# Moving deferred stores from ScalarE's to SyncE's queue, and cutting GpSimd's 1024-column sums in two

## The chip, the cores and the metric

The kernel runs on one core of one Trainium2 chip. The metric is device time in microseconds (us) of that core. A profile of one execution goes with each kernel. All runs that are compared here are of the fast state; the granted TensorE clock is told where it matters.

The engines' names: TensorE is PE in the profile (its weight loads PEld), VectorE is DVE, ScalarE ACT, GpSimd POOL, SyncE SP. "SPq" and "ACTq" are the sequencers of SyncE and ScalarE, which issue the DMAs, in order: when one issue waits, the later ones stand behind it (12.3 us at SyncE in the changed kernel). A DMA lands when its data have arrived; in the kernel before, the 718 DMAs of SyncE landed in the order of their issue, and so did the 202 of ScalarE. In this program TensorE writes its results into PSUM; a bank is a part of PSUM, which VectorE or ScalarE reads out before the program lets TensorE use it again. The other tiles lie in SBUF. The profile also tells the clock that TensorE was granted, as a share of full speed; a stretch at 0.5 is called a half-clock stretch here (in own_by_scalar matmuls stood 0.42 us apart in one, in place of 0.216).

## The reference, cut to what matters

Two blocks follow each other. A lightning attention with decay over (4, 8, 768, 64) gives x of 3072 tokens by 512. Then four experts work on every token:

```python
p = domain_probs / (domain_probs.sum(-1, keepdims=True) + 1e-09)
for e in range(4):
    h = np.maximum(x @ w1[e], 0.0)        # 512 -> 1024
    out += p[:, e:e + 1] * (h @ w2[e])    # 1024 -> 512
```

All is float32. The expert products are over 95% of the multiplications.

## The kernel before

The products are made by Winograd's form of Strassen's scheme, partly in two levels: seven products of sums of blocks in place of eight products. So sums of blocks of x, w1 and w2 ("operands") are needed. They are made once, on GpSimd and VectorE, stored to DRAM tensors (`x_ops`, `w1_ops`, `w2_sums`, `w2_ops`), and loaded again for each group of tokens. Three groups (`g`) of 1024 tokens times four experts make twelve units; a unit has seven first products (x with w1) and seven second ones (hidden with w2), whose matmuls alternate on TensorE.

Work that is not urgent goes through two queues in the program: `chores` make sums, and `stores` holds the DMAs that write them. A store is issued two pumps after its sums were put into the program, so that its data should be ready by then:

```python
def pump():
    for f in older:
        f()
    older[:] = stores
    stores.clear()
    if chores:
        chores.pop(0)()
```

The stores are on ScalarE's queue (one of several places):

```python
s = stage.tile([P, 4, 256], FP32, name="ops", tag="st")
for i, (name, x, y, op) in enumerate(ops):
    b[name] = s[:, SLOT[name]]
    tt(eng, b[name], b[x], b[y], op)              # 4 sums of 256 columns
stores.append(lambda: (
    nc.scalar.dma_start(out=to[:, 0], in_=blk[:, 0, 0:256]),
    nc.scalar.dma_start(out=to[:, 1:5], in_=s[:]),
    nc.scalar.dma_start(out=to[:, 5:7], in_=blk[:, 1].rearrange("p (a f) -> p a f", a=2)),
    made.add(what),
))
```

ScalarE also copies TensorE's results out of PSUM and applies the Relu. The loads are on SyncE's queue (`nc.sync`), written into the program one product ahead; `xs_in` and `ws_in` have two buffers each, `w2t` six. The outer sums of w1, w2 and x are one GpSimd instruction of 1024 columns each:

```python
def total(name, a, b, op):
    t = stage.tile([P, 2, W], FP32, name="w1o", tag="st")   # W = 512
    tt(nc.gpsimd, t[:], st[a][:], st[b][:], op)
    st[name] = t
```

For the first group and the second expert (seven pairs of operands) the sums are both stored and used at once by TensorE; `keep_own` makes these stores, three for x and three for w1 in each pair, 42 DMAs. I call them the own stores.

## Time and profile before

| | before |
|---|---|
| median of the first 3 runs | 1215.12 us (1214.82 to 1217.88) |
| span of the profiled run | 1211.4 us |
| TensorE busy | 1186.9 us, 98% |
| VectorE, ScalarE, GpSimd busy | 66%, 22%, 51% |
| DMA issues by SyncE and by ScalarE | 718 and 202 |
| TensorE's gaps over 0.15 us, summed | 20.8 us, of these 9.7 us from 53 to 669 us |

Two views carry the reading: TensorE's waits (who waited, for whom, us in total, times, longest) and the timeline around each wait. The prediction shows their lines. With TensorE at 98%, the busy shares of the others say nothing of what an edit is worth; the list of TensorE's few gaps does.

### The profile page before, as it was taken

Reading aid. Unit: us, or ns where it says so; the run is one execution under the profiler, and the core shown is the slowest. Engines: PE = TensorE matmul, PEld = TensorE weight load, DVE = VectorE, ACT = ScalarE, POOL = GpSimd, SP = SyncE. Lnnn points to the kernel's source line nnn. Section 1 sums busy time; section 2 is a strip of 40 time slices with the busy share of each in tenths; the row PEclk is TensorE's granted clock in tenths of the full one; section 3 lists DMA queues with packets and bytes.
Section 4 is the critical chain, followed back from the end, with each engine's and each line's share of the span. In section 5 each row is a group of like instructions: output and inputs, shape, how many; then the busy total and the mean of one; then the engine's idle time right before and its main releaser. Section 6 shows DMA issues by size and latency. Waiting matters only on the chain.

```text
span 1211.4 us, 17782 instructions
## 1 busy us (share of the span) xinstructions
PE 1186.9 (98%) x6593; PEld 1024.2 (85%) x6593; DVE 802.2 (66%) x1313; ACT 261.7 (22%) x476; POOL 622.8 (51%) x548
## 2 busy tenths in 40 slices
PE   7999999999999999999999999999999999999998
PEld 6788888888888888888888888888888888888877
DVE  5587686478567846746764874764665667777774
ACT  3322112112212211321211120120143241241132
POOL 4556247466366800015624655405665774873873
PEclk9999999999999999999999999999999999999999
DMA  9578489999999875679987998988986657566542
GB/s 234 155 274 270 168 279 316 367 311 317 350 338 320 282 264 188 221 246 292 293 288 239 293 315 318 333 288 258 326 301 235 238 202 268 198 258 209 204 170 74
DMA packets 227446, 317.93 MB, mean 262 GB/s; under 512 B 91648, under 2 KB 168864, under 8 KB 227360
## 3 DMA queue, kind: packets, MB, share of 16 engines
q1 hardware_dynamic: 191840, 257.08, 64.3%
q10 hardware_dynamic: 35520, 59.72, 13.4%
q8 instruction: 52, 0.85, 0.3%
q14 instruction: 34, 0.28, 0.1%
HBM read 231.40 MB, written 85.34 MB: 261 GB/s over the span
## 4 chain that ended last, share of the span: by engine, by line
PE 89%; DVE 5%; DMA 2%; SPq 1%; ACT 1%; issue 0%; POOL 0%; ACTq 0%; DVEq 0%
PE pg L701 38%; PE q L755 30%; PE pq L926 13%; DVE m L94 2%; PE sp L455 2%; PE op L483 2%; PE op L478 1%; PE pM L1016 1%; DVE hS L94 1%; DVE xt L94 1%; SPq L110 1%; PE kp L432 1%; PE op L491 1%; PE qp L432 1%; PE pM L896 1%
## 5 line engine op out<-in xcount | busy, mean ns | idle before, releaser
L701 PE MATMUL pg<-xs_in,ws_in 128*128 128x256 f32 x1960 | 473.7, 382 | 3.2 <-DVE m L94 2.5
L701 PEld LDWEIGHTS pg<-xs_in,ws_in 128*128 128x128 f32 x1960 | 367.4, 190 | 62.2 <-DVE m L94 9.9
L94 DVE TENSOR_TENSOR m<-pg,m 128x512 f32<-128x512 f32 x451 | 307.6, 688 | 134.1 <-PE pg L701 122.4
L755 PE MATMUL q<-w2t,hS 128*128 128x256 f32 x1024 | 242.5, 380 | 0.0
L755 PEld LDWEIGHTS q<-w2t,hS 128*128 128x128 f32 x1024 | 193.9, 190 | 26.7
L771 DVE SCALAR_TENSOR_TENSOR acc<-q,gate,acc 128x256 f32<-128x256 f32 x192 | 92.5, 482 | 147.6 <-PE q L755 147.1
L755 PE MATMUL q<-w2t,m 128*128 128x256 f32 x768 | 181.7, 379 | 0.0
L755 PEld LDWEIGHTS q<-w2t,m 128*128 128x128 f32 x768 | 145.4, 190 | 20.0
L713 ACT ACTIVATE m<-m 128x512 f32<-128x512 f32 x132 | 82.9, 632 | 348.2 <-DVE m L94 308.2
L94 POOL TENSOR_TENSOR kn<-kn,s_decay 128x512 f32<-128x512 f32 x20 | 21.5, 1074 | 204.7 <-PE kp L432 193.3
L94 POOL TENSOR_TENSOR m<-m,xT 128x512 f32<-128x512 f32 x64 | 81.2, 1288 | 73.9 <-ACT m L713 52.3
L94 DVE TENSOR_TENSOR sums<-pq,sums 128x256 f32<-128x256 f32 x154 | 64.6, 422 | 46.8 <-PE pq L926 41.9
L926 PE MATMUL pq<-acc,w2t 128*128 128x256 f32 x352 | 86.6, 379 | 0.0
L94 DVE TENSOR_TENSOR m<-m,m 128x512 f32<-128x512 f32 x96 | 84.6, 887 | 0.0
L709 ACT COPY m<-pg 128x512 f32<-128x512 f32 x88 | 51.0, 587 | 141.9 <-PE pg L701 128.9
L926 PEld LDWEIGHTS pq<-acc,w2t 128*128 128x128 f32 x352 | 66.7, 190 | 9.6 <-issue 0.6
L94 POOL TENSOR_TENSOR ops<-w2b 128x256 f32<-128x256 f32 x24 | 17.4, 745 | 98.3 <-DMA w2b<-in_moe_w_dram 66.9
L648 ACT ACTIVATE m<-m 128x512 f32<-128x512 f32 x48 | 30.4, 632 | 149.0 <-DVE m L94 149.0
L94 POOL TENSOR_TENSOR acc<-hT,hT 128x512 f32<-128x512 f32 x32 | 40.2, 1271 | 30.8 <-PE pq L926 21.4
L94 DVE TENSOR_TENSOR hS<-m,m 128x512 f32<-128x512 f32 x64 | 49.6, 779 | 5.6 <-ACT m L713 5.6
L94 POOL TENSOR_TENSOR w2o<-w2b 128x1024 f32<-128x1024 f32 x16 | 39.6, 2480 | 19.2 <-DMA w2b<-in_moe_w_dram 9.6
L94 POOL TENSOR_TENSOR ops<-w1o 128x256 f32<-128x256 f32 x32 | 29.7, 947 | 30.1 <-PE pg L701 20.5
(126 smaller groups left out, 1328.4 us busy)
## 6 DMA issues: line engine op xcount, KB each, us to landing
xs_in<-x_ops SPq DMA_DIRECT2D x70, 896.0 KB, 5.0
ws_in<-w_ops SPq DMA_DIRECT2D x70, 896.0 KB, 8.1
w2t<-w_ops SPq DMA_DIRECT2D x66, 256.0 KB, 6.9
w2t<-w_sums SPq DMA_DIRECT2D x64, 256.0 KB, 5.2
w_ops<-ops ACTq DMA_DIRECT2D x28, 512.0 KB, 5.5
w2t<-in_moe_w_dram SPq DMA_DIRECT2D x48, 256.0 KB, 5.0
x_ops<-ops ACTq DMA_DIRECT2D x17, 512.0 KB, 7.8
w2b<-in_moe_w_dram SPq DMA_DIRECT2D x32, 256.0 KB, 5.9
```

The source lines that it names most:

```text
L94: eng.tensor_tensor(out=o, in0=a, in1=b, op=op)
L110: nc.sync.dma_start(out=to[:, :, r], in_=of[:, :, r])
L432: nc.tensor.transpose(out=x[:, ac * C:(ac + 1) * C], in_=y[:, 2 * ac:2 * ac + 2].rearrange("p r d -> p (r d)"), identity=ident[:],)
L455: nc.tensor.matmul(out=sp[r][:, ac * C:(ac + 1) * C], lhsT=hc(kT)[half[r], ac], rhs=hc(qT)[half[r], ac], start=True, stop=True,)
L483: nc.tensor.matmul(out=op[r][half[x], a * C:(a + 1) * C], lhsT=vn[:, 4 * r + 2 * a + x], rhs=hc(st[r])[:, 2 * a + x], start=(first and a = ...
L648: nc.scalar.activation(out=o[:], in_=o[:], func=AF.Relu)
L701: nc.tensor.matmul(out=p[:, j * 256:(j + 1) * 256], lhsT=ws[i][:, j * P:(j + 1) * P], rhs=xs[i], start=(fresh and j == 0), stop=True, skip ...
L709: nc.scalar.copy(out=new[at][:], in_=p[:])
L713: nc.scalar.activation(out=new[at][:], in_=new[at][:], func=AF.Relu)
L755: nc.tensor.matmul(out=p[:, s * DH:(s + 1) * DH], lhsT=h[A_OF[m]][:, c * 256 + s * P:c * 256 + (s + 1) * P], rhs=fed2[g, e, m][uu][:, c], ...
L771: nc.vector.scalar_tensor_tensor(out=o, in0=x, scalar=w, in1=o, op0=ALU.mult, op1=ALU.add)
L926: nc.tensor.matmul(out=p[:, 0:256], lhsT=fed3[e, m, x // 2][:, x % 2, c * P:(c + 1) * P], rhs=b[B_OF[i]][:, c * 256:(c + 1) * 256], start= ...
```

## The change

The intent: ScalarE should not issue stores, because its copies stand behind them, and a VectorE sum should not take 2.60 us beside a GpSimd sum where it takes 0.68 us alone. All deferred stores go to SyncE, and 52 GpSimd sums of 1024 columns become 104 of 512.

```diff
+    def halves(o, a, b, op):
+        for i in range(2):
+            tt(nc.gpsimd, o[:, i], a[:, i], b[:, i], op)
...
         stores.append(lambda: (
-            nc.scalar.dma_start(out=to[:, 0], in_=blk[:, 0, 0:256]),
-            nc.scalar.dma_start(out=to[:, 1:5], in_=s[:]),
-            nc.scalar.dma_start(out=to[:, 5:7], in_=blk[:, 1].rearrange("p (a f) -> p a f", a=2)),
+            nc.sync.dma_start(out=to[:, 0], in_=blk[:, 0, 0:256]),
+            nc.sync.dma_start(out=to[:, 1:5], in_=s[:]),
+            nc.sync.dma_start(out=to[:, 5:7], in_=blk[:, 1].rearrange("p (a f) -> p a f", a=2)),
             made.add(what),
         ))
...
-            tt(nc.gpsimd, t[:], st[a][:], st[b][:], op)
+            halves(t[:], st[a][:], st[b][:], op)
...
-                nc.scalar.dma_start(out=to[:, x:y], in_=of)
+                nc.sync.dma_start(out=to[:, x:y], in_=of)
```

Cut here: the same two edits at the sums of w2 and x, at the stores of `w2_sums` and at those of the finished rows of `out`.

More of the change, by code (lines that the diff above doesn't have):

```diff
@@ L223, in total @@
             flat = [x[:].rearrange("p u c d -> p (u c d)") for x in (t, st[a], st[b])]
-            tt(nc.gpsimd, *flat, op)
+            halves(*(x[:].rearrange("p u c d -> p u (c d)") for x in (t, st[a], st[b])), op)
             stores.append(lambda: (
-                nc.scalar.dma_start(out=w2_sums[e, n].rearrange("p u w -> p (u w)"), in_=flat[0]),
+                nc.sync.dma_start(out=w2_sums[e, n].rearrange("p u w -> p (u w)"), in_=flat[0]),
                 made.add(("w2", e, name)),
@@ L271, in total @@
             t = stage.tile([P, 2, 2, DH], FP32, name="w2o", tag="st")
-            tt(nc.gpsimd, *(x[:].rearrange("p q c d -> p (q c d)") for x in (t, st[a], st[b])), op)
+            halves(*(x[:].rearrange("p q c d -> p q (c d)") for x in (t, st[a], st[b])), op)
             st[name] = t
@@ L289, in total @@
             t = stage.tile([P, 2, W], FP32, name="xo", tag="st")
-            tt(nc.gpsimd, t[:], a, b, op)
+            halves(t[:], a, b, op)
             st[name] = t[:]
@@ L772, in part @@
             if e == E - 1 and m in ("M2", "M4", "M5", "M3"):
-                stores.append(lambda: nc.scalar.dma_start(out=out[n * P:(n + 1) * P, j * DH:(j + 1) * DH], in_=o))
+                stores.append(lambda: nc.sync.dma_start(out=out[n * P:(n + 1) * P, j * DH:(j + 1) * DH], in_=o))
         def done():
```

## The prediction

> **What bounds the kernel now.** I read the page's part 1 and part 5 first, then the waits of TensorE, then the timeline at each place where TensorE stands still.
>
> ```profile
> PE 1186.9 (98%) x6593; PEld 1024.2 (85%) x6593; DVE 802.2 (66%) x1313; ACT 261.7 (22%) x476; POOL 622.8 (51%) x548
> ```
>
> TensorE is busy for 1186.9 of 1211.4 us. Its mark of "busy" is no illusion here: I took the distance from one 128x256 matmul to the next in the trace, and 4808 of about 4960 are 0.21 to 0.22 us. So at most 24.5 us (2.0% of the span) can be won by any change that leaves the matmuls alone, and this one does: the order of instructions on TensorE holds the same work before and after. Adding up the gaps over 0.15 us in TensorE's timeline gives 20.8 us. Of them 7.8 us lie before 26 us (the first loads, two of the copies), and 3.2 us after 1156 us (the tail); the change touches neither. 9.7 us are left between 53 and 669 us. What ends each gap, from the waits of TensorE:
>
> ```profile
> PE pg L701 <- DVE m L94: 4.8, 6, 1.7
> PE pg L701 <- ACT m L709: 2.8, 2, 2.1
> PE pM L1016 <- DVE xt L94: 1.2, 1, 1.2
> ```
>
> Columns: waiter and what it waited for, us in total, times, longest. ScalarE and VectorE are 22% and 66% busy and yet late at these moments: something else holds them up. Two pieces of timeline show what. First the largest stall, in the chain of waits of the stretch 92 to 104 us (start, length, what):
>
> ```profile
> 95.30 0.33 ACT m L1028
> ...
> 98.09 0.48 ACTq L995
> 98.56 0.05 issue
> 98.61 1.15 ACT m L1028 x2
> 99.76 0.48 ACT m L709
> 100.24 0.14 issue
> 100.38 1.97 PE pg L701 x8
> ```
>
> ScalarE issues six stores in a row (0.33 to 0.72 us each), and the two Relus and the PSUM copy that TensorE needs stand behind them. TensorE idles 2.14 us. Then one of VectorE's, in the timeline of 241 to 249 us:
>
> ```profile
> 244.02 2.34 POOL L94 TENSOR_TENSOR w1o<-w1b 128x1024 f32<-128x1024 f32 x1
> ...
> 244.31 2.60 DVE L94 TENSOR_TENSOR m<-m,m 128x512 f32<-128x512 f32 x1
> ...
> 246.84 1.27 DVE L94 TENSOR_TENSOR m<-pg,m 128x512 f32<-128x512 f32 x2
> 247.57 1.59 PEld L701 LDWEIGHTS pg<-xs_in,ws_in 128*128 128x128 f32 x8 [0.77 <-DVE m L94]
> ```
>
> The same VectorE sum takes 0.68 us when GpSimd is quiet. Here it starts 0.3 us after a GpSimd sum of 1024 columns and ends 0.55 us after that one ends; the next VectorE operation, which frees TensorE's bank, is late.
>
> [...] ScalarE's 202 issues take 97 us, 0.48 us each. [...]
>
> **The change part by part.** Stores: 195 of ScalarE's 202 issues go to SyncE (718 become 913 in the built order). ScalarE gets back about 195 x 0.48 = 94 us of sequencer time, nearly all beside other work. On TensorE's path I count:
> - the stall at 98.2 us, 2.1 us, goes;
> - at 200.7 us a copy from PSUM stands behind a store that waited for GpSimd: 0.6 us, goes;
> - at 185.6 us the chain is stores, late copy of qT at 182.15, VectorE's qs, late m: 0.6 us, goes.
> Together 3.3 us.
>
> Halves: GpSimd runs 52 sums of 1024 columns (32 w2o, 12 w1o, 8 xo) at about 2.47 us; they become 104 of 512 columns. The rows of 512 columns take 1.27 to 1.36 us, so 104 x 1.3 = 135 us in place of 128, 7 us more on an engine with half its time free. A blocked VectorE sum then waits at most 1.27 us: where a 512-column GpSimd pair met VectorE at 95.2 us, the pair stretched to 3.46 us and VectorE's sum took 1.16 us, so VectorE does get in between. At the four stalls that show a 1024-column sum beside a slow VectorE sum (247.2: 0.37, 277.7: 0.41, 409.0: 1.42, 668.5: 0.29 us) VectorE gains about 1.0 us each time: the three small ones vanish and 409 keeps 0.4, so 2.1 us. At 58.7 us (1.2 us) the first xt sum also waits for a 1024-column sum, but would arrive just after the second half has started; I count 0.5. Together 2.6 us.
>
> What it costs: SyncE runs ahead of the others, and its queue is in order. A store placed there waits for its data with all later loads behind it. In the built order of the changed kernel six stores of the first pair of operands stand directly before the four loads of the first w2t tiles. Before:
>
> ```profile
> 81.86 3.29 SPq L736 DMA_DIRECT2D w2t<-in_moe_w_dram  x4
> ...
> 91.55 0.96 SPq L110 DMA_DIRECT2D qn<-in_q_dram  x2
> ```
>
> These loads land 7.4 us later in the median, at 89 to 91 us, and TensorE reads them from 96.3 us. The second of the six stores needs VectorE's four ops sums, which end at 92.3 us (VectorE is paced by TensorE there, so they come no earlier than some 91). Then five issues at 0.5 us, and the first two loads leave at 94.8 and 95.5 us, with 1.7 MB of stores ahead of them[...]: 4 us at the 400 GB/s this stretch reaches. They land at about 100 to 102 us. TensorE, which now comes to that point a little short of 96.3 us, waits some 4.5 us (3 to 7). That takes the place of the 2.1 us stall just counted, and it is the one loss that I can put a place to.
>
> For the other loads I compared, one by one, how long before TensorE's first use each landed with how late the stores ahead of it would let it go. Several slip by 4 to 19 us (w2t and xs_in between 165 and 216 us), but they had 9 to 30 us in hand or their stores are ready earlier than before, since GpSimd no longer waits for ScalarE to free its buffers. Between 300 and 400 us the DMA engines are full and some ws_in loads land with 0.1 to 3.3 us to spare[...]. I add 0.5 us.
>
> Sum: 1215.1 - 3.3 - 2.6 + 4.5 + 0.5 = 1214.2 us, called 1214.5.
>
> **The rivals.** (1) ScalarE was the hidden culprit and SyncE has time: all of 3.3 + 2.6 us is won, nothing lost, perhaps 2 us more from VectorE's other late moments (173.3 us). For it: SyncE's issues take about 379 us of 1211, and the six stores' data other than VectorE's are ready at 83 us. Against: the order in SyncE's queue. It would make 1207 to 1209 us. (2) The queue of SyncE becomes the bound: each product's xs_in and ws_in loads come one product ahead (12 to 15 us), and stores that wait for GpSimd[...] make many of them late. For it: SyncE already waits 217.6 us for TensorE at the xs_in loads, so it has no lead beyond two buffers, and the DMA share is 95 to 100% from 300 to 400 us. Against: nearly all loads had over 4 us in hand. With 1 to 2 us in ten products it would make 1225 to 1232 us. (3) VectorE, relieved of blocking, is hardly on TensorE's path and the halves give nothing: 1217 us.
>
> **Range and chances.** The floor is 1215.1 - 9.7 = 1205 us if every stall between 53 and 669 us went; the three runs of before spread by 3 us. I take 1209 to 1221 us. 2% is 24.3 us: faster by that is more than all idle time of TensorE that the change can reach, 1%. Slower by that needs rival 2 at its worst, 4%. Within 2%: 95%.
>
> **What would show it.** Right: ScalarE without store issues; no wait of TensorE for ScalarE's m at 98 and 200 us; TensorE idle for 3 to 7 us at about 96 us behind a w2t load that left after 94 us; GpSimd with 104 more sums of 512 columns and 5 to 10 us busier; the mean of VectorE's m<-m,m of 128x512 down from 887 ns; TensorE's waits for VectorE's m down from 4.8 to under 3 us. Wrong: no wait for w2t near 96 us (then rival 1), or repeated waits for xs_in or ws_in (rival 2), or VectorE's sums as slow as before[...] (rival 3).

## The result, and the profile after

| | before | after |
|---|---|---|
| median (6 runs each) | 1215.52 us (1212.97 to 1220.06) | 1210.89 us (1209.25 to 1212.63) |
| ratio | | 0.9958, 95% interval 0.9938 to 0.9979 |
| span of the profiled run | 1211.4 us | 1207.5 us |
| TensorE's gaps, summed | 20.8 us | 16.6 us |

A ratio here is the mean time of one kernel's fast runs over that of the other's fast runs of the same rounds, so it isn't quite the ratio of the medians. The time lies inside the predicted range (1209 to 1221 us), 3.6 us under the predicted 1214.5, and the class is "same", as forecast. All runs were correct.

Part 1 of the page of the changed kernel:

```profile
PE 1187.3 (98%) x6593; PEld 1028.4 (85%) x6593; DVE 792.4 (66%) x1313; ACT 262.1 (22%) x476; POOL 635.0 (53%) x600
```

GpSimd has 52 instructions more and is 12.2 us busier, VectorE is 9.8 us less busy with the same 1313 instructions: it is blocked for less time (the mean of its m<-m,m fell from 887 to 832 ns, as shown below). The waits of TensorE in the changed kernel:

```profile
PE pg L706 <- DVE m L94: 2.5, 5, 1.2
PE q L760 <- DMA w2t<-in_moe_w_dram: 2.1, 1, 2.1
...
PE pg L706 <- DMA ws_in<-w_ops: 1.0, 2, 0.6
...
PE pM L1021 <- DVE xt L94: 0.4, 1, 0.4
```

The wait for ScalarE's copies (2.8 before) is gone. That for VectorE's m is about halved (4.8 before), that for xt fell from 1.2 to 0.4. Two new ones have come, both for loads that SyncE issued late. The chain of waits of the changed kernel from 92 to 106 us shows the larger one:

```profile
93.52 0.57 SPq L1000
...
94.13 0.46 SPq L1000
...
94.63 4.34 DMA w2t<-in_moe_w_dram
98.97 0.14 issue
99.11 1.97 PE q L760 x8
```

Six stores leave SyncE before the load of the first w2t tile, which before left at 81.86 us and now at 94.63. It lands 4.34 us later, and TensorE, ready at 97.0 us, starts at 99.1. SyncE's own waits (us in total, times, longest) say what it stood for:

```profile
SPq L1000 <- DVE ops L94: 24.9, 3, 12.3
```

The longest of these three waits is that for VectorE's four sums of the first pair: for 12.3 us SyncE issued nothing, and the DMA engines ran dry behind it (from 86 to 92 us they moved 0 GB/s; in the kernel before, the loads of w2t were under way then, at 212 GB/s). The stores, no longer in the way of ScalarE's copies, now hold up what stands behind them in SyncE's queue.

The other part of the change, in the timeline of 241 to 248 us (start, length):

```profile
246.40 2.94 POOL L94 TENSOR_TENSOR w1o<-w1b 128x512 f32<-128x512 f32 x2
246.47 1.74 DVE L94 TENSOR_TENSOR m<-m,m 128x512 f32<-128x512 f32 x1
```

It is the w1 sum that the prediction shows at 244 us. GpSimd's two halves take 2.94 us in place of 2.34, and VectorE's sum 1.74 us in place of 2.60: it starts 0.07 us after the first half and ends 0.55 us after that one's end, and the second half takes 1.71 us where the first took 1.26. Over all 96 such VectorE sums the mean fell, in the groups by shape (first before, then after; busy us, mean ns):

```profile
L94 DVE TENSOR_TENSOR m<-m,m 128x512 f32<-128x512 f32 x96 | 84.6, 887 | 0.0
```

```profile
L94 DVE TENSOR_TENSOR m<-m,m 128x512 f32<-128x512 f32 x96 | 79.3, 832 | 0.0
```

In the kernel before, 48 of the 96 have no GpSimd sum or product beside them and take 0.68 us in the mean; the other 48 take 1.09 us, and the eight that start while a 1024-column sum is running 1.44 to 2.84 us; each of the eight ends 0.54 to 0.55 us after that GpSimd sum. VectorE's m<-pg,m, which reads one input from PSUM, takes 0.69 us in the mean with one beside it (255 cases) and without (196).

One more difference between the two profiles has nothing to do with the change: at 23 us TensorE waits for a load of q, 1.7 us in the run before and 0.2 us in the run after. Profiles of other runs have 0.2 to 3.9 us there. To keep it out, I also give for each profile the time from TensorE's first transpose for chunk 5 (at about 33 us) to the end; the expectations call it "from the fifth turn". It is 1178.5 us before and 1174.6 us after.

### The profile page after: what moved, and what is told of

Read it like the earlier page. It is cut to its first block, busy times and chain, and to the rows that moved or that the text cites. A ratio compares the mean times of both kernels' runs of the same rounds, so it can differ in the third digit from the quotient of the medians.

```text
span 1207.5 us, 17884 instructions
## 1 busy us (share of the span) xinstructions
PE 1187.3 (98%) x6593; PEld 1028.4 (85%) x6593; DVE 792.4 (66%) x1313; ACT 262.1 (22%) x476; POOL 635.0 (53%) x600
## 4 chain that ended last, share of the span: by engine, by line
PE 92%; DVE 3%; DMA 2%; SPq 2%; issue 1%; ACT 0%; DVEq 0%
PE pg L706 38%; PE q L760 30%; PE pq L931 13%; PE pM L1021 3%; PE op L488 2%; PE sp L460 2%; DMA ws_in<-w_ops 1%; PE op L483 1%; DVE m L94 1%; SPq L115 1%; PE kp L437 1%; PE qp L437 1%; PE op L496 1%; DVE hS L94 1%; PE pM L901 1%
## 5 line engine op out<-in xcount | busy, mean ns | idle before, releaser
L94 DVE TENSOR_TENSOR m<-m,m 128x512 f32<-128x512 f32 x96 | 79.3, 832 | 0.0
L94 POOL TENSOR_TENSOR ops<-w2b 128x256 f32<-128x256 f32 x24 | 18.3, 783 | 104.2 <-DMA w2b<-in_moe_w_dram 92.9
L94 DVE TENSOR_TENSOR hS<-m,m 128x512 f32<-128x512 f32 x64 | 52.5, 824 | 5.6 <-ACT m L718 5.6
L94 POOL TENSOR_TENSOR w2o<-w2b 128x512 f32<-128x512 f32 x32 | 42.2, 1341 | 13.0 <-DMA w2b<-in_moe_w_dram 11.2
L94 POOL TENSOR_TENSOR acc<-hT,acc 128x512 f32<-128x512 f32 x32 | 40.7, 1270 | 7.4 <-PE pq L931 5.4
```

The lines of the kernel that those rows point to most:

```text
L94: eng.tensor_tensor(out=o, in0=a, in1=b, op=op)
```

## The experiments

My theory after the result: the two parts add. The halves win because VectorE's sums are blocked for less time. The stores win at ScalarE what they lose at SyncE. Rivals: all of the gain is from the stores, or from something else that halving does.

Twelve runs were made (one of them, after_again, is the changed kernel once more), in three calls; those of one call shared a chip. Summary (the ratio is to the kernel before on the same chip; the last column is one profile's time from chunk 5 on, 1178.5 us before):

| run | median us | ratio | 95% interval | from chunk 5 |
|---|---|---|---|---|
| halves_only | 1211.04 | 0.9952 | 0.9937 to 0.9968 | 1173.5 |
| stores_only | 1215.89 | 0.9997 | 0.9986 to 1.0008 | 1179.6 |
| early_w2t | 1208.90 | 0.9933 | 0.9918 to 0.9949 | 1174.0 |
| own_by_scalar | 1217.13 | 1.0000 | 0.9989 to 1.0010 | 1180.3 |
| quarters | 1212.37 | 0.9978 | 0.9961 to 0.9994 | 1176.2 |
| halves_w2 | 1214.07 | 0.9992 | 0.9984 to 0.9999 | 1178.2 |
| halves_w1_x | 1212.53 | 0.9974 | 0.9964 to 0.9983 | 1177.6 |
| own_by_sync | 1208.78 | 0.9948 | 0.9931 to 0.9965 | 1173.1 |
| after_again | 1210.46 | 0.9945 | 0.9924 to 0.9966 | 1177.3 |
| start_after | 1209.34 | 0.9941 | 0.9923 to 0.9960 | 1177.5 |
| best | 1207.22 | 0.9923 | 0.9904 to 0.9942 | 1174.3 |
| split_stores | 1220.72 | 1.0043 | 1.0030 to 1.0056 | 1189.7 |

### halves_only: the sums cut, the stores left with ScalarE

```diff
 # against the changed kernel
-            nc.sync.dma_start(out=to[:, 0], ...)      # and all other moved stores
+            nc.scalar.dma_start(out=to[:, 0], ...)    # the halves stay
```

> The halves alone, stores stay with ScalarE. My theory (the parts add: the halves remove TensorE's waits behind VectorE sums that a 1024-column sum blocks, 2.1 to 2.6 us): ratio to the kernel before 0.998 (about 1212.9 us); in the trace no TensorE gap above 0.2 us at about 247, 277 and 668 us, at most 0.4 us at 409 us, while the gaps at 98 us (2.1 us, released by ScalarE), 185 and 200 us (0.6 us each) stay. Rival, the gain is all of the moved stores: ratio 1.000 and the four gaps stay. Rival, the gain is all of the halves: ratio 0.996.

Measured: 0.9952, so 5.8 us (3.9 to 7.7). That is nearest to the second rival's 0.996, and over twice what I had put on the halves. The waits of TensorE in this run:

```profile
PE pg L706 <- ACT m L714: 2.9, 2, 2.1
PE pg L706 <- DVE m L94: 1.4, 2, 1.2
```

ScalarE's two waits are still there as in the kernel before, and VectorE's are down from six to two. The gaps at 247, 277 and 668 us are gone and 409 us has 0.2 us left, as expected; but 59 us (1.23 to 0.46), 174 us (1.69 to 1.19) and 185 us (0.59 to none) shrank too. Since 20 us of span are lost to gaps in all, I can add them up: 4.0 us less than before after the start, of the 5.0 us by which the time from chunk 5 fell.

How a blocked sum costs time far from itself is seen at 174 us. Some 10 us before that wait VectorE meets a w1 sum (first before, then halves_only):

```profile
164.72 2.35 POOL L94 TENSOR_TENSOR w1o<-w1b 128x1024 f32<-128x1024 f32 x1 [1.84 <-PE pg L701]
165.28 2.08 DVE L94 TENSOR_TENSOR kv<-kv,q_decay 128x256 f32<-128x256 f32 x1
```

```profile
165.88 2.68 POOL L94 TENSOR_TENSOR w1o<-w1b 128x512 f32<-128x512 f32 x2 [1.84 <-PE pg L706]
166.45 0.99 DVE L94 TENSOR_TENSOR kv<-kv,q_decay 128x256 f32<-128x256 f32 x1
```

From there to the end of TensorE's wait VectorE is idle for no more than 0.1 us at a time in either trace, so the 1.1 us that kv no longer loses come through in order; 0.6 us of them are lost again to slower sums between (xt takes 3.14 us in place of 2.73, one m 0.84 in place of 0.68), and the wait is 0.5 us shorter.

### stores_only: the stores moved, the sums whole

```diff
     def halves(o, a, b, op):
-        for i in range(2):
-            tt(nc.gpsimd, o[:, i], a[:, i], b[:, i], op)
+        tt(nc.gpsimd, o, a, b, op)
```

> The stores alone, sums of 1024 columns stay whole. My theory: the three ScalarE gaps (2.1, 0.6, 0.6 us) go, a wait for the first w2t tiles of about 2 us at 97 us comes, the VectorE gaps at about 247, 277, 409 and 668 us stay (2.5 us together); ratio 0.998 to 0.999 (1213 to 1214 us). Rival, all of the gain is of the stores: ratio 0.996 with the VectorE gaps gone too.

Measured: 0.9997, 0.4 us faster with an interval from 1.7 us faster to 1.0 slower: nothing. The waits of TensorE:

```profile
PE pg L705 <- DVE m L94: 5.3, 7, 1.7
PE q L759 <- DMA w2t<-in_moe_w_dram: 2.1, 2, 1.6
```

The w2t wait is there, ScalarE's are gone, VectorE's stayed in sum (5.3 us; 4.8 before), though not all at their old places. Of the four small VectorE gaps only 409 us stood unchanged at its place (1.41 us); 247 and 277 us were gone and others of 0.2 to 0.5 us had come at 688 and 702 us, and one of 0.8 us for ws_in at 351 us. Gaps under half a microsecond come and go from kernel to kernel; a single one of them proves nothing.

With these two runs the result is settled to first order: halves 0.9952, stores 0.9997, product 0.9949, and the changed kernel measured 0.9958 and, in a second call on another chip, 0.9945.

### early_w2t: the first w2t loads ahead of the own stores

```diff
     for m in SEQ0[2:]:
+        if m == "M4":
+            feed2(0, 0, "M1")
+            feed2(0, 0, "M2")
         for x, f in enumerate(direct_product(0, m, blocks, ...)):
```

> The changed kernel, with the loads of the first two products' w2t tiles put before the last of the seven direct products, so that SyncE issues them ahead of the six stores that wait for VectorE. My theory (the 2.1 us wait at 97 us is the in-order queue of SyncE): TensorE's wait for w2t is gone, ratio to the kernel before 0.994 (2 us below the changed kernel's, about 1209 us). Rival, something else stands right behind it (VectorE's backlog or ScalarE's Relus at 94 to 98 us): a gap of 1 to 2 us released by DVE or ACT takes its place and the ratio stays at 0.996.

Measured: 0.9933, near the forecast 0.994, with the lowest median of this call. The wait for w2t is gone. But the rival has a part in it: TensorE now waits 1.2 us for a copy of ScalarE at 99.8 us, in the timeline of 96 to 102 us:

```profile
99.69 0.63 ACT L1033 ACTIVATE m<-m 128x512 f32<-128x512 f32 x1 [0.57 <-DVE m L94]
...
100.23 1.05 ACT L714 COPY m<-pg 128x512 f32<-128x512 f32 x2
...
100.94 1.10 PE L706 MATMUL pg<-ops 128*128 128x256 f32 x4 [1.19 <-ACT m L714]
```

No store is in ScalarE's way here; its Relu waits for VectorE, which is some 4 us behind TensorE at this point. So of the 2.1 us of the w2t wait about 0.9 us could be had at this place, and the profile's time from chunk 5 is only 0.6 us under that of the changed kernel (a gap for ws_in at 227 us also grew from 0.4 to 1.3 us). The rest of the lower ratio is within the intervals, which also overlap with that of halves_only (0.9937 to 0.9968): that moving the stores adds anything to the halves isn't shown.

### own_by_scalar: the own stores back to ScalarE, the rest with SyncE

```diff
             for (x, y), of in pieces:
-                nc.sync.dma_start(out=to[:, x:y], in_=of)
+                nc.scalar.dma_start(out=to[:, x:y], in_=of)
```

> The changed kernel, but the stores of the pairs of operands that are used at once (the seven first, 43 DMAs) go back to ScalarE. My theory: the w2t wait at 97 us is gone and the ScalarE wait of 2.1 us at 98 us is back, so the ratio stays within 0.0015 of the changed kernel's 0.996. Rival, ScalarE's stores there cost more than the one visible gap: ratio 0.998 or above. Rival, SyncE's wait costs more: ratio 0.994.

(They are 42 DMAs; this text on record counts one too many, and so does that of own_by_sync.) Measured: 1.0000. I had expected 0.996 and the rivals named 0.998 or 0.994: a clear miss. The w2t wait is gone and ScalarE's 2.15 us at 102 us is back, as I said; but a new gap of 4.3 us has come at 188.6 us. Its chain of waits, 181 to 193 us:

```profile
183.36 4.45 DMA w_ops<-w1o
...
187.88 0.33 ACTq L1000
...
188.25 0.76 ACTq L1000
...
189.10 0.59 ACT qT L442
...
189.72 0.69 DVE qs L94
...
192.01 0.69 DVE m L94
...
192.83 0.77 PE pg L706
```

A store of ScalarE (L1000) is released by the landing of another DMA, of other data, that SyncE issued at 183.36 us. That DMA lands at 187.81 us, 4.45 us after its issue, and the store leaves at 187.88. The traces of the kernel before and of the changed one show the same pattern: in each, the 920 DMA issues name eight landing semaphores, 115 each, and none of the 912 issues that come after another on the same semaphore starts before that other DMA has landed. In the kernel before, 243 of these issues come after a DMA of the other issuer and 59 start within 0.1 us after its landing (some may be chance); in the changed one it is 13 and 1. So in this chain ScalarE's store waits for a store of SyncE, and SyncE's issues for GpSimd (its sums end at 182.96 us, SyncE issues from 182.97); behind them stands the copy of qT, behind it VectorE's qs, and TensorE's bank comes free 4.3 us late. From 191.7 us, 1.1 us before the gap ends, the granted clock is 0.5 for 6.8 us (twelve matmuls at 0.42 us distance in place of 0.216), which costs another 2.5 us. Together this is 6.8 us; the time from chunk 5 is 5.7 us longer than the changed kernel's, whose 1.0 us of waits for ws_in this run doesn't have.

### quarters: four pieces of 256 columns

```diff
 # against halves_only
-        for i in range(2):
-            tt(nc.gpsimd, o[:, i], a[:, i], b[:, i], op)
+        for i in range(4):
+            x = i // 2, slice(i % 2 * W // 2, (i % 2 + 1) * W // 2)
+            tt(nc.gpsimd, o[:, x[0], x[1]], a[:, x[0], x[1]], b[:, x[0], x[1]], op)
```

> Stores stay with ScalarE, the sums of 1024 columns in four pieces of 256. The theory now (VectorE's sums with two SBUF inputs wait for the GpSimd instruction that is running, and the length of that instruction is what counts): the remains at about 61 us (0.46), 174 us (1.19) and 408 us (0.21) shrink further, by 0.5 us or less in all, since most of 174 us comes from sums of 256 columns; ratio 0.9945 to 0.9955 where halves alone gave 0.9952. GpSimd 5 to 15 us busier than with halves. Rival (the gain is of something else that halving changes once, such as the form of the access): the same gaps as with halves to 0.05 us, ratio unchanged. Rival (GpSimd's fixed cost for an instruction begins to tell): the sums of operands come late, gaps behind POOL or DMA, ratio above 0.997.

(The trace of the kernel before has the wait: the eight m<-m,m that start during a 1024-column sum of GpSimd take 1.44 to 2.84 us in place of 0.68, and each ends 0.54 to 0.55 us after that sum.) Measured: 0.9978, which misses the forecast on the slow side and lies in the band of the last rival (above 0.997). VectorE's blocking itself behaves as expected: VectorE's m<-m,m has a mean of 804 ns (863 with halves, same stores), VectorE is 12.7 us less busy, and the gap at 408 us is gone. But the gap at 61 us grew (0.77 us; 0.46 with halves), GpSimd is 18.6 us busier than with halves (655.0 against 636.4 us; 5 to 15 expected), and where ScalarE's stores wait for it, TensorE now waits longer, in the timeline of 197 to 206 us:

```profile
203.80 0.33 ACTq L160 DMA_DIRECT2D w_ops<-ops  x1
...
204.66 0.59 ACT L715 COPY m<-pg 128x512 f32<-128x512 f32 x1 [4.62 <-PE q L761]
...
205.29 0.92 PE L707 MATMUL pg<-xs_in,ws_in 128*128 128x256 f32 x3 [1.48 <-ACT m L715]
```

The same gap is 0.79 us with halves. And this profile has a half-clock stretch that the one of halves_only lacks. The stretches 104 to 108 us of both (columns: length, busy us of PE, PEld, DVE, ACT, POOL, granted clock, DMA share, GB/s), quarters first:

```profile
104.00:108.00 4.00, 4.00 (x13) 3.21 (x12) 3.06 (x7) 0.59 (x1) 0.00 (x0) 0.57 1.12 337
```

```profile
104.00:108.00 4.00, 4.00 (x20) 3.54 (x19) 4.00 (x8) 0.00 (x0) 1.76 (x2) 1.00 1.00 289
```

TensorE is "busy" for 4.00 us in both and does 13 matmuls in one, 20 in the other. The stretch begins 1.3 us after the end of a gap of 2.13 us behind ScalarE, which both kernels have (2.14 us with halves). The runs of quarters also spread by 11.6 us. In this one profile 1.2 of the 2.6 us that it loses to halves_only from chunk 5 on are gaps and 1.6 us are matmul time, where the half-clock stretch lies; over the 13 executions I can't tell GpSimd's added time and the clock apart. That shorter pieces unblock VectorE further is shown, that they pay is not.

### halves_w2 and halves_w1_x: which sums matter

```diff
 # halves_w2: w1 and x whole again            # halves_w1_x: the two sums of w2 whole again
-            halves(t[:], st[a][:], st[b][:], op)
+            tt(nc.gpsimd, t[:], st[a][:], st[b][:], op)
```

> Of the sums of 1024 columns only the 32 of w2 in halves, the 12 of w1 and 8 of x whole, stores with ScalarE. The theory (each gap belongs to the sum that runs at its place): the gaps at about 59 us (1.23 to 0.46) and 668 us (0.29 to none) shrink as in halves alone, those at 185, 247, 277 and 409 us stay; ratio 0.9985 to 0.9995, and from the fifth turn to the end 1177 us where the kernel before has 1178.5 and halves alone 1173.5. Rival (the halves of any kind shift GpSimd's whole schedule): gaps at places of w1 and x sums go as well, ratio below 0.997.

> The complement: the 20 sums of w1 and x in halves, those of w2 whole, stores with ScalarE. The theory: the gaps at 185, 247, 277 us (w1) and 409 us (x) go or shrink to 0.2, those at 59 and 668 us stay; ratio 0.996 to 0.997, from the fifth turn to the end 1175 us; the gains of this run and of the run with w2 alone add up to that of halves alone within the intervals. Rival: as above, the parts don't add.

Measured: 0.9992 for w2 alone, as forecast, and 0.9974 for w1 and x, just outside the forecast 0.996 to 0.997. The two gains are 0.0008 and 0.0026, in sum 0.0034, and those of all halves 0.0048 with an interval from 0.0032: they add within the intervals. The single profiles don't: from chunk 5 they are 0.4 and 0.9 us shorter than before, halves_only 5.0. The larger gaps go with their own sums in every profile: 59 us is 1.2 us with w2 whole and 0.45 with w2 halved; 409 us is 1.4 us with x whole and 0.2 with x halved; 174 us is 1.7 us with w1 whole and 1.2 with w1 halved (w1 and x were halved together, so which of the two a gap belongs to is read from the sum on the timeline). The small ones didn't: 185, 247 and 277 us, expected to stay, were gone with w1 whole too, which is half of the rival's sign; its ratio, below 0.997, didn't come. And both single profiles (1178.2 and 1177.6 us from chunk 5) have chance items in them: a half-clock stretch at 101.6 us in the first, a 0.9 us gap at 379 us in the second; the second misses its 1175 us by 2.6, which that gap doesn't cover.

### own_by_sync: halves, and only the own stores moved

```diff
 # the changed kernel, with early w2t loads, and
-            nc.sync.dma_start(out=to[:, 0], ...)      # and all stores but the own ones
+            nc.scalar.dma_start(out=to[:, 0], ...)
```

> Halves, the 43 stores of the seven first pairs with SyncE, all other stores with ScalarE as in the kernel before, and the first w2t loads moved ahead of them. If only those stores stood before ScalarE's copies at the costly place: the 2.1 us gap at 98 us is 1.2 us at most, no ws_in gap at 227 us (1.3 us in the run with early w2t), the 0.8 us gap at 200 us stays; ratio 0.993 to 0.9945, as fast as early_w2t (0.9933) or faster. Rival (ScalarE and SyncE hold each other up when both store, as in the run where only these stores stayed with ScalarE, which lost 4.3 us at 188 us and stood at 1.000): a gap of 2 us or more at a new place behind an ACT copy, ratio above 0.996.

Measured: 0.9948, a little short of the 0.993 to 0.9945 expected (it holds with the interval, 0.9931 to 0.9965), with a median of 1208.78 us. ScalarE's gap at 98 us is 0.7 us, there is no ws_in gap at 227 us, and the 0.8 us at 200 us is gone, which I had expected to stay. No large new gap came, unlike in the mirror case; a VectorE gap of 1.0 us stands at 103 us. With the w2t loads first, moving the 42 own stores gave the same median as moving all 195 (1208.90 in early_w2t, on another chip). Neither is clear of halves_only, which moves none (0.9937 to 0.9968).

### split_stores: ScalarE's stores doubled

The kernel before, the six stores of the first pair in twelve pieces.

```diff
             for (x, y), of in pieces:
-                nc.scalar.dma_start(out=to[:, x:y], in_=of)
+                n = 128 if what[1:] in ((0, "M1"), (1, "M1")) else 256
+                for f in range(0, 256, n):
+                    nc.scalar.dma_start(out=to[:, x:y, f:f + n], in_=of[:, :, f:f + n])
```

> The kernel before, with the six stores of the first pair of operands cut into twelve, still with ScalarE: the suspected cost doubled. Theory (stores stand in ScalarE's order before the copies that TensorE waits for, some 0.5 us each[...]): the gap at 98 us grows from 2.1 to 4.5 to 6 us and a half-clock stretch of 3.4 us follows in every profile; ratio 1.003 to 1.005. Rival (the copies wait for VectorE and the stores only fill the time): the gap stays at 2.1 us and the ratio at 1.000.

Measured: 1.0043, as forecast. ScalarE's timeline from 95 to 112 us:

```profile
97.40 0.81 ACTq L997 DMA_DIRECT2D x_ops<-xT  x2
98.25 1.00 ACTq L997 DMA_DIRECT2D x_ops<-ops  x2
...
102.62 1.23 ACTq L997 DMA_DIRECT2D w_ops<-w1b  x2
103.90 1.15 ACT L1030 ACTIVATE m<-m 128x512 f32<-128x512 f32 x2 [5.88 <-DVE xt L94]
104.96 1.05 ACT L709 COPY m<-pg 128x512 f32<-128x512 f32 x2
```

Twelve issues fill 97.4 to 103.9 us, the two Relus and the two copies follow at once, and TensorE's gap is 5.3 us (2.1 before); the granted clock is 0.5 for 6.8 us, twice the expected length (which is that of the stretch in quarters, 3.41 us), from 1.6 us before its end. The profiled execution is the slowest of the 13 (1225.02 us) and has longer gaps elsewhere too, such as 2.4 us for ws_in at 387 us, so the ratio and not this profile is the measure. So the stores, not a wait for VectorE, held ScalarE up at this place, and "5.88 <-DVE xt" on the Relu's line is only the last semaphore seen before it: ScalarE was issuing.

### after_again, start_after, best

```diff
 # start_after: the changed kernel, and        # best: own_by_sync, and the same edit
+    load(4)
     raw_w1(0, "A21")
     raw_w1(0, "A22")
...
-        if i + 4 < CPG:
+        if 0 < i < CPG - 4:
             load(i + 4)
```

> The changed kernel itself, unchanged, to stand on the same chip as the next two. Ratio 0.995 to 0.9965 (0.9958 before). What it costs or saves beside the kernel with halves alone (0.9952 on another chip) is within the intervals.

> The changed kernel with the loads of the fifth chunk put ahead of the last two blocks of w1. The theory: in the profiles so far TensorE waits 0.2 to 3.9 us at 23 us for that chunk's q[...]; this start, which no version touched, is most of the spread of 3 to 8 us between runs of one kernel. Expected: that gap below 0.3 us, the spread of the runs below 3 us, ratio 0.001 to 0.003 under after_again's. Rival, the spread comes from elsewhere: it stays at 4 us or more.

> Halves, the stores of the seven first pairs with SyncE and the first w2t loads ahead of them, all other stores with ScalarE, and the fifth chunk's loads earlier. If the gains add: ratio 0.991 to 0.9935, about 1206 us, no half-clock stretch before the end. If not: as own_by_sync, 0.9948.

Measured on one chip: 0.9945, 0.9941 and 0.9923. The changed kernel again was a hair under its forecast band. With chunk 4 loaded earlier (the expectation calls it the fifth chunk) the gap at 23 us is gone, and the six runs lie within 1.7 us (1208.46 to 1210.13) where after_again's lie within 5.8 and the 18 runs of the kernel before within 7.1. That the start was most of the spread isn't shown: halves_only without this edit lies within 2.3 us, and best, which has it, within 3.5. The median fell by 1.1 us, which the intervals can't confirm. A half-clock stretch came at 96.8 us in its profile. The best version has a median of 1207.22 us, 8.5 us under the kernel before on its chip, and its runs (1205.58 to 1209.08) all lie below those of the kernel before (1213.68 and up); its 0.9923 is inside the forecast. No half-clock stretch came before the end in its profile. It beats the kernel before clearly, yet by less than 1%. Against the changed kernel on that chip the means are 1207.1 and 1210.4 us, while the intervals overlap; its time from chunk 5 (1174.3) is no shorter than that of halves_only (1173.5).

## Why the prediction was right or wrong, point by point

**The ceiling.** Right. With gaps of 9.7 us in reach, nothing could move the time by 2%; even the best version stayed at 0.8%.

**The stores' gain at ScalarE, 3.3 us.** The mechanism is right (in split_stores more stores make a longer gap, as ordered, and ScalarE's waits of 2.1 us at 98 us and 0.6 at 200 us are gone in the profile after). But 2.1 us was too much for the first: early_w2t has neither stores nor late loads there, and TensorE still waits 1.2 us, since VectorE is behind. So at most some 0.9 us were the stores' own. Another term was put in the wrong place: the 0.6 us at 185 us went in halves_only with all stores still at ScalarE, so it was not ScalarE's alone.

**The stores' cost at SyncE, 4.5 us for w2t and 0.5 us for the DMA queue.** The event came where I said, behind the load I named: issued at 94.63 us (I had 94.8), with the six stores before it. Its size was off: 2.1 us, outside the "3 to 7". The step that failed is "with 1.7 MB of stores ahead of them (...) They land at about 100 to 102 us": the load took 4.34 us and landed at 98.97. The stores had begun to move as they were issued, from 91.85 us: 300 GB/s from 92 to 94.63 us are some 0.8 MB, so about 0.9 MB were left ahead of the load. How much these delayed the load, no run isolates: the last store landed at 97.72 us and the load 1.25 us after it, in the order of issue. And TensorE came to the point at 97.0 us, later than "a little short of 96.3 us", having lost 0.9 us to VectorE just before. The ws_in loads lost 1.0 us in two gaps (I had 0.5), at 227 and 258 us rather than between 300 and 400. (A slip in the reading that changes nothing: the four loads of before land at 90.2 to 92.1 us and not at 89 to 91, after 7.3 to 8.3 us.)

Together I had the stores at +1.7 us (-3.3 + 4.5 + 0.5); stores_only measured -0.4 (-1.7 to +1.0), so +1.7 lies a little outside. That this part came near is partly luck: its two large terms, 2.1 and 4.5 us, were both more than twice what could be had or was lost there (0.9 and 2.1), and they stand against each other in the sum.

**The halves' gain, 2.6 us.** This is the term that was mis-sized, and it makes the difference to 1210.9: halves_only measured 5.8 us (3.9 to 7.7). The step as put: "At the four stalls that show a 1024-column sum beside a slow VectorE sum (...) so 2.1 us. At 58.7 us (...) I count 0.5." At those five places the gain was 3.1 us (1.07 for the three small, 1.2 at 409 us, 0.8 at 59 us). What I left out are places where the blocked VectorE sum lies some microseconds upstream of the wait: 174 us lost 0.5 us although sums of 256 columns stand beside it (the lines are shown at halves_only), and 185 us lost 0.6, with a cause that halves_w2 leaves open. With 0.15 us lost at 200 us that makes 4.0 us of the profile's 5.0. Most of the last 1.0 us is in how gaps are read: a matmul before a gap is drawn 0.379 us long, where the next one usually starts after 0.216, so each gap is read some 0.16 us too short. By the distances from matmul to matmul over 0.5 us, the stalls from chunk 5 on fell by 4.7 us. VectorE's instructions follow each other without a break there (from 165.3 us to the end of TensorE's wait at 175.0 us it is idle for 0.1 us at most at a time in the kernel before), so a blocked sum delays what is behind it; VectorE's busy time fell by 7.8 us in halves_only, of which the sums next to a wait are only a part.

**The signs asked for.** Seen: no store issues at ScalarE, no wait of TensorE for its m at 98 and 200 us, the w2t wait (2.1 us, short of the 3 to 7 asked for), m<-m,m below 887 ns, waits for VectorE's m under 3 us. GpSimd is 12.2 us busier, not 5 to 10: the groups of its halves have means of 1.27 to 1.5 us where I had counted with 1.3. The kernel before already had four such sums at 1.55, which the prediction left out; in the pairs that are shown the added time goes with VectorE's coming between.

**The rivals.** "ScalarE was the hidden culprit" falls: moving its stores alone is worth nothing. "SyncE becomes the bound" showed only in small: 3.1 us of waits for loads. "The halves give nothing" is the reverse of the truth.

## What to carry to other kernels

Read a blocked engine's cost along its whole queue, not only where the critical engine happens to be waiting: halving the blocking instructions won about twice what I had read from the gaps at their sides. A store put into an in-order queue is a wait for its data (12.3 us of SyncE here); whether the copies of one engine or the loads of another stand behind it is the choice to make, and urgent loads go into the program ahead of such stores (early_w2t removed the wait, though its gain in time is within the noise). Before counting a wait as a gain, ask what would hold the engine up next: of 2.1 us only 0.9 could be had here. When one engine is at 98%, first sum its gaps: an edit that leaves its work alone can win little more.

## What the profiles show of clock, queues and memory

- The granted clock. The half-clock stretches, those at the end of the program aside, last 3.41 us (quarters from 104.2 us; the mean granted clock from 104 to 108 us is 0.57) or twice that (own_by_scalar from 191.7 us; 0.83 from 180 to 200 us), with 0.42 us between matmuls in place of 0.216. Of the 22 gaps of TensorE from 1.46 to 2.40 us in the 14 profiles, seven had a half-clock stretch that began during the gap or within 1.5 us after it (in quarters a gap of 2.13 us at 100.8 us, the stretch from 104.2 us), and 15 had none (halves_only with 2.14 us at 99.4 us; split_stores twice with 2.36 us). All four gaps of 3.39 us or more had one (4.3 us in own_by_scalar and 5.3 us in split_stores are two of them). What decides it between these lengths, no run shows; an estimate of the loss is half of the 3.41 us, 1.7 us.
- The issuer of a DMA. What the choice of the issuer did here is mostly to set which work stands behind a waiting store. One store's wait held SyncE for 12.3 us, and TensorE then waited 2.1 us; 0.48 us for an issue (ScalarE's 202 took 97 us) was the smaller matter. In own_by_scalar a store of ScalarE also waited for the landing of SyncE's DMA (4.45 us from issue to landing, 4.3 us lost by TensorE).
- The order of landing. In the changed kernel the stores and the load behind them landed in the order of issue, the last store at 97.72 us and the load at 98.97, as did all 913 DMAs of SyncE. How much the stores delayed the load, no run isolates: the first two such loads took 8 us in the kernel before, but with 324 GB/s moved from 82 to 88 us at a DMA share of 0.99, while here the DMA engines had moved nothing from 86 to 92 us.
- VectorE beside GpSimd. VectorE's sum took 2.60 us beside a 1024-column sum and 1.74 us beside two halves, and the GpSimd pair stretched from 2.34 us (as one) to 2.94 us.
